# Attention and soft mixture of experts on one core: room for loads by the work of a block of instructions

## The chip, the cores and the metric

The kernel runs on one core of a Trainium2 chip. The metric is the time of one execution on the device in microseconds (us), the median over timed runs. A trace of one more execution was taken by the hardware profiler. TensorE, which multiplies matrices, appears there as PE (matmuls) and PEld (loads of weights); VectorE is DVE, ScalarE is ACT, GpSimd is POOL, and SyncE, whose queue issues every transfer of this kernel, is SP.

## What is computed

The first half is attention with a local window, for 8 batches and 8 heads of width 64: 512 local positions and 32 global ones.

```python
k_all = concatenate([k_g, k_l], axis=2); v_all = concatenate([v_g, v_l], axis=2)
s_g = scale * q_g @ k_all.T                     # 32 global rows see all keys
out_g = softmax(s_g) @ v_all
s_ll = where(abs(pos_q - pos_k) <= 32, scale * q_l @ k_l.T, -1e9)
s_l = concatenate([scale * q_l @ k_g.T, s_ll])  # local rows: global keys and a band
out_l = softmax(s_l) @ concatenate([v_g, v_l])
x = concatenate([out_g, out_l], axis=2)         # 4608 rows of 512
```

The second half is a soft mixture of 8 experts with 4 slots each, on all 4608 rows:

```python
logits = x @ phi                                # 4608 x 32
slot_input = softmax_over_rows(logits).T @ x    # 32 x 512
slot_out[e] = relu(slot_input[e] @ w1[e]) @ w2[e]
out = softmax_over_slots(logits) @ slot_out
```

## The kernel before, in words

The attention is a loop of 32 steps (L550), one for each pair of heads of a batch, four steps to a batch. A step makes the scores of its pair on TensorE, finishes the values of the pair two steps back, turns the exponentials of the pair one step back, and has parts of the logits, slot sums and global rows of earlier batches between them. Which of these a step has depends on its place in the batch, so the steps of a batch differ from one another, and each batch repeats the one before it. After the loop come the slots' experts: 64 pages of weights of 512 KB each (`w1` and `w2`, all of 32 MB), of which up to 30 have room of their own and can be loaded during the loop; the others follow after it, into room that the attention gives back. Then the results are combined and written out.

All loads are issued by SP, in the order of the program. The transfers of a load are held back by a wait on one TensorE instruction: `behind(d, i)` (L101) makes the load wait for instruction `i`. Which load waits for which instruction is settled while the program is built, by `begin_loads` (L105). TensorE's instructions are counted (`counted`, L89: a matmul in f32 counts 4, one in bf16 or a transpose 2, since each becomes that many loads of weights and matmuls), and each time the count passes a multiple of 256, `begin_loads` adds `ROOM` = 1040 KB to the room that is left and chooses a set of waiting loads. It takes all that are due by the next step and, beside them, up to three others, so that the sum of sizes comes as near to the room as it can, in classes of 200 KB. What is left over or overdrawn, up to 300 KB, goes to the next choice. A group of 256 TensorE instructions is called a **block** below.

The sizes in KB stand in the program: keys of two pairs (`k`) 736, values of two pairs (`v`) 780, queries of one pair (`q`) 256, global queries of a batch (`qg`) 64, a page of weights (`w`) 512. Each load has a due step, one step or more before its first use; loads of pages have none inside the loop.

Of the kernel before, what the change touches and what calls it, by code (L numbers as in the profile page):

```python
# [2 lines left out]

# [6 lines left out]
BF16 = mybir.dt.bfloat16  # L10
# [39 lines left out]
ROOM = 1040  # L50
SPARE = 300


def window(c):

    w = min(max(c, 1), 14)
    return ((w - 1) % 3, (w - 1) // 3)
# [9 lines left out]
def kernel(  # L67
# [12 lines left out]
    nc = tc.nc  # L80
# [4 lines left out]
    pe = [OFFSET]  # L85
    lines = [[], []]
    room, step = [0], [0]

    def counted(i, n):  # L89
        pe[0] += n  # L90
        if pe[0] // 256 > (pe[0] - n) // 256:
            begin_loads(i)
        return i

    def mm(out, lhsT, rhs, **flags):
        return counted(nc.tensor.matmul(out, lhsT, rhs, **flags), 2 if lhsT.dtype == BF16 else 4)  # L96

    def flip(out, x, idn):
        return counted(nc.tensor.transpose(out, x, idn), 2)  # L99

    def behind(d, i):  # L101
        tc.add_manual_dep(d.ins, i.ins.name, mybir.DependencyInfo(
            mybir.DependencyClass.Sync, mybir.DependencyReason.DATA))

    def begin_loads(i):  # L105

        lines[0].sort(key=lambda load: load[1])
        room[0] += ROOM
        near = [load for load in lines[0] if load[1] <= step[0] + 1]
        rest = [load for load in lines[0] if load not in near] + lines[1][:2]  # L110
        sets = [near + list(more) for n in range(4) for more in combinations(rest, n)]
        best = min(sets, key=lambda s: (abs(sum(load[0] for load in s) - room[0]) // 200, sum(load[1] for load in s)))
        for entry in best:
            lines[entry in lines[1]].remove(entry)
            room[0] -= entry[0]
            for d in entry[2]():
                behind(d, i)
        room[0] = max(min(room[0], SPARE), -SPARE)

    def begin_due(k):  # L120

        lines[0].sort(key=lambda load: load[1])
        while lines[0] and lines[0][0][1] <= k:
            size, due, load = lines[0].pop(0)
            room[0] -= size
            load()
# [111 lines left out]
    def scores(k):  # L238
        pool, tag = (psV, "v") if k == 1 else (psS, "s")
        ps = pool.tile([P, 2, 4, P], F32, tag=tag, name=f"s{k}")  # L240
        for i in (0, 2):
            for r in range(2):
                mm(ps[32 * i:32 * i + 64, r], idm[64 * r:64 * r + 64, :], mk[64 * r:64 * r + 64, i:i + 4, :],
                   start=True, stop=False)
        for t in range(4):
            for i in range(4):
                c = 4 * t + i
                for r in range(2):
                    mm(ps[32 * i:32 * i + 32, r, t, :], qs[k][64 * r:64 * r + 64, 32 * c:32 * c + 32],
                                     key_window(k, r, c), start=False, stop=(t == 3))  # L250
        sc[k] = ps
# [283 lines left out]
    def line_up(kind, j):  # L535
        if j < (B if kind == "qg" else NK) and (kind, j) not in lined:
            lined.add((kind, j))
            size, load = {"k": (736, load_k), "q": (256, load_q), "v": (780, load_v), "qg": (64, load_qg)}[kind]
            due = {"k": min(j - 1, NK - 3), "qg": min(4 * j + 2, NK - 3), "q": j - 1, "v": j + 1}[kind]
            lines[0].append((size, due, lambda: load(j)))  # L540
# [5 lines left out]
    def do_logits(b, pl):  # L546
        lgs[b] = new_logits(b)
        nc.scalar.copy(lgs[b][:, 0, :], pl)

    for k in range(NK):  # L550
        b, s = k // 4, k % 4
        step[0] = k
        begin_due(k)
        scores(k)
        line_up("q", k + 3)
        if k == 0:
            line_up("k", 4)
            line_up("v", 2)
            line_up("v", 4)
            line_up("qg", 0)  # L560
            lines[1].extend((512, NK, load_page) for _ in range(NWA))

        if k > 1:
            values(k - 2)
        shift(k)
        if k - 1 in GS:
            global_shift(GS.index(k - 1))
        if k - 2 in GS:
            global_values(GS.index(k - 2))
            for j in (k + 1, k + 3):  # L570
                line_up("v", j)
        if k in GS:
            global_scores(GS.index(k))
            line_up("qg", b + 1)
            for j in (k + 3, k + 5):
                line_up("k", j)
        if s == 0 and b > 1:
            slot_sums(b - 2)
        if s == 2 and b:
            pl = psT.tile([P, P], F32, tag="t", name=f"pl{b - 1}")  # L580
            logits_mm(pl, b - 1, range(4))
            do_logits(b - 1, pl)
        if k == 19:
            pl = psT.tile([P, P], F32, tag="t", name="plg")
            logits_g_mm(pl, 0)
            lgs["g", 0] = new_logits("g0")
            nc.scalar.copy(lgs["g", 0][G, 0, :], pl[G])
        if k == 21:
            pag = psT.tile([P, DM], F32, tag="t", name="pag")
            for g in range(2):  # L590
                slot_sums_g(0, pag, g)
        if k > 1:
            normalise(k - 2)
        if k in GS:
            global_max(GS.index(k))

        if k:
            transpose_exp(k - 1)
        if k - 1 in GS:
            global_transpose(GS.index(k - 1))  # L600
        if s == 3 and b:
            turn(b - 1, ALL)
        if k == 20:
            turn(("g", 0), G)
        if k == 18:
            turn_xg(0)
        if k > 2 and s != 2:
            turn_x(k - 3)
        if k > 2 and s == 1:
            turn_x(k - 2)  # L610
        if k == NK - 1:
            make_v(k)
        if k:
            make_v(k - 1)
        if k - 2 in GS:
            global_normalise(GS.index(k - 2))
        if s == 2 and b:
            dispatch_max(b - 1, ALL)
            dispatch_exp(b - 1, ALL)
        if s == 3 and b:  # L620
            dispatch_total(b - 1, ALL)
            combine_max(b - 1)
            combine_exp(b - 1)
        if k == 19:
            dispatch_max(("g", 0), G)
            dispatch_exp(("g", 0), G)
        if s == 0 and b > 1:
            add_sums(b - 2, pa[b - 2], ALL)
            combine_sum(b - 2, cTs[b - 2].rearrange("p (t s) -> p t s", s=NS))
        if k == 21:  # L630
            dispatch_total(("g", 0), G)
            add_sums(("g", 0), pag, G)
            combine_max(("g", 0))
            combine_exp(("g", 0))
        if k == 22:
            combine_sum(("g", 0), cg[:, 0:1, :])
# [85 lines left out]
    for g in range(2):  # L722
        c = slice(256 * g, 256 * g + 256)
        p = (pa7, pb7)[g]
# [228 lines left out]
```

## Time and profile before

| what | value |
|---|---|
| median of 3 timed runs (lowest to highest) | 278.23 us (277.56 to 280.18) |
| the profiled execution's own time | 276.72 us |
| its span, first to last instruction | 274.7 us |
| PE matmul busy | 247.9 us, 90% of the span |
| DVE, ACT, POOL busy | 167.3, 112.9, 98.6 us |
| transfers by SP's queue | 76.64 MB |
| mean rate of all transfers | 282 GB/s |
| chain of waits: PE / transfers / issue | 70% / 19% / 4% |

The span runs from the first to the last instruction of the program. A busy time is the time in which at least one instruction of that engine runs. "Issue" in the chain of waits is time in which an engine waited for nothing that the profile shows: no semaphore, no other engine, no transfer of the kernel's own. Transfers that fetch instructions for an engine are listed under queues of their own (q8 and q14), beside q1, which carries the kernel's data.

### The profile page before, as it was taken

Reading aid. Unit: us, or ns where it says so; the run is one execution under the profiler, and the core shown is the slowest. Engines: PE = TensorE matmul, PEld = TensorE weight load, DVE = VectorE, ACT = ScalarE, POOL = GpSimd, SP = SyncE. Lnnn points to the kernel's source line nnn. Section 1 sums busy time; section 2 is a strip of 40 time slices with the busy share of each in tenths; the row PEclk is TensorE's granted clock in tenths of the full one; section 3 lists DMA queues with packets and bytes.
Section 4 is the critical chain, followed back from the end, with each engine's and each line's share of the span. In section 5 each row is a group of like instructions: output and inputs, shape, how many; then the busy total and the mean of one; then the engine's idle time right before and its main releaser. Section 6 shows DMA issues by size and latency. Waiting matters only on the chain.

```text
span 274.7 us, 13972 instructions
## 1 busy us (share of the span) xinstructions
PE 247.9 (90%) x6348; PEld 174.3 (63%) x6348; DVE 167.3 (61%) x336; ACT 112.9 (41%) x254; POOL 98.6 (36%) x174
## 2 busy tenths in 40 slices
PE   7599989999999899899999989989899999998740
PEld 5477856777687577777777866758786344553520
DVE  0769757767967695596789767858554234044440
ACT  0317425623644483357337426726454001133330
POOL 0345654454546436334555563435710000000000
PEclk9979999999999999999999999999999999999995
DMA  7967786768677867695867496687789999999997
GB/s 216 391 222 248 230 296 209 259 222 296 199 242 262 296 206 237 229 333 168 285 218 292 146 342 205 233 237 255 243 278 412 409 410 407 410 407 383 351 353 253
DMA packets 29275, 77.53 MB, mean 282 GB/s; under 512 B 2592, under 2 KB 12192, under 8 KB 29216
## 3 DMA queue, kind: packets, MB, share of 16 engines
q1 hardware_dynamic: 29216, 76.64, 79.3%
q8 instruction: 50, 0.82, 1.2%
q14 instruction: 9, 0.07, 0.1%
HBM read 67.72 MB, written 8.91 MB: 279 GB/s over the span
## 4 chain that ended last, share of the span: by engine, by line
PE 70%; DMA 19%; issue 4%; DVE 1%; ACT 1%; SPq 0%
DMA w<-in_w_dram 18%; PE s L96 17%; PE o L96 14%; PE t L99 12%; PE xt L99 5%; PE og L96 4%; PE tg L99 3%; PE gm L96 3%; PE pl L96 3%; PE pc L96 2%; PE pa L96 2%; DMA con<-in_cst_dram 1%; PE gs L96 1%; ACT o L828 1%; PE po L96 1%
## 5 line engine op out<-in xcount | busy, mean ns | idle before, releaser
L258 DVE TENSOR_REDUCE mx<-s 128x8 f32<-128x1024 f32 x32 | 39.1, 1223 | 42.3 <-PE s L96 42.2
L222 POOL COPY va<-v 128x650 f32<-128x650 f32 x31 | 22.5, 726 | 82.5 <-PE o L96 67.6
L270 ACT ACTIVATE e<-t 128x512 f32<-128x512 f32 x64 | 35.0, 599 | 41.4 <-PE t L99 41.2
L260 DVE TENSOR_TENSOR e<-s,mx 128x1024 f32<-128x1024 f32 x32 | 39.2, 1225 | 6.6 <-PE o L96 2.3
L96 PE MATMUL s<-k,q 64*32 64x128 f32 x2048 | 38.8, 276 | 4.8 <-issue 4.1
L96 PE MATMUL o<-v,e 128*32 128x65 f32 (+1 forms) x640 | 42.0, 224 | 0.0
L96 PE MATMUL o<-va,e 128*64 128x65 f32 (+1 forms) x620 | 39.6, 225 | 0.0
L96 PEld LDWEIGHTS s<-k,q 64*32 64x32 f32 x2048 | 29.3, 106 | 13.2 <-issue 12.1
L96 PEld LDWEIGHTS o<-v,e 128*32 128x32 f32 (+1 forms) x640 | 33.1, 115 | 6.5 <-issue 5.5
L99 PE MATMUL t<-con,e 128*128 128x128 f32 x256 | 36.2, 285 | 1.0 <-issue 0.5
L99 PEld LDWEIGHTS t<-con,e 128*128 128x128 f32 x256 | 28.1, 143 | 13.0 <-ACT sg L320 5.9
L96 PEld LDWEIGHTS o<-va,e 128*64 128x64 f32 (+1 forms) x620 | 31.8, 115 | 2.1
L96 PE MATMUL o<-vb,e 128*32 128x65 f32 x496 | 27.8, 221 | 1.8 <-issue 1.8
L96 PEld LDWEIGHTS o<-vb,e 128*32 128x32 f32 x496 | 22.2, 109 | 2.5 <-issue 2.5
L300 DVE TENSOR_TENSOR xh<-o,r 128x512 f32<-128x512 f32 x32 | 22.1, 691 | 1.9 <-PE pa L96 0.5
L223 POOL COPY va<-v 32x650 f32<-32x650 f32 x31 | 22.3, 719 | 1.9
L224 POOL COPY vb<-v 64x520 f32<-64x520 f32 x31 | 19.1, 618 | 1.8
L225 POOL COPY vb<-v 64x520 f32<-64x520 f32 x31 | 18.9, 611 | 1.7
L99 PE MATMUL xt<-con,xh 128*128 128x128 f32 x128 | 19.1, 278 | 0.3 <-ACT e L270 0.2
L384 ACT COPY xT<-xt 128x512 f32<-128x512 f32 x32 | 18.6, 606 | 0.6 <-PE xt L99 0.4
L828 DVE COPY o<-pc 128x512 f32<-128x512 f32 x16 | 10.3, 686 | 11.5 <-PE pc L96 11.5
L828 ACT COPY o<-pc 128x512 f32<-128x512 f32 x16 | 8.6, 589 | 20.7 <-PE pc L96 20.7
(179 smaller groups left out, 367.5 us busy)
## 6 DMA issues: line engine op xcount, KB each, us to landing
w<-in_w_dram SPq DMA_DIRECT2D x64, 512.0 KB, 8.1
v<-in_vS_dram SPq DMA_DIRECT2D x15, 780.0 KB, 5.0
k<-in_kT_dram SPq DMA_DIRECT2D x14, 736.0 KB, 5.5
q<-in_qT_dram SPq DMA_DIRECT2D x32, 256.0 KB, 3.4
out_dram<-o SPq DMA_DIRECT2D x16, 512.0 KB, 6.4
k<-in_kT_dram SPq DMA_DIRECT2D x4, 368.0 KB, 5.4
v<-in_vS_dram SPq DMA_DIRECT2D x2, 390.0 KB, 6.5
qg<-in_qG_dram SPq DMA_DIRECT2D x8, 64.0 KB, 2.3
```

Source lines behind the costliest of these rows:

```text
L96: return counted(nc.tensor.matmul(out, lhsT, rhs, **flags), 2 if lhsT.dtype == BF16 else 4)
L99: return counted(nc.tensor.transpose(out, x, idn), 2)
L222: nc.gpsimd.tensor_copy(va, v[:, 0:5])
L223: nc.gpsimd.tensor_copy(va[0:32], v[0:32, 1:6])
L224: nc.gpsimd.tensor_copy(vb[64:128], v[64:128, 0:4])
L225: nc.gpsimd.tensor_copy(vb[0:64], v[0:64, 1:5])
L258: nc.vector.reduce_max(mx, ps, axis=AX.X)
L260: nc.vector.tensor_tensor(e, ps, bc(mx, P), ALU.subtract)
L270: nc.scalar.activation(es[k][:, r], pt, AF.Exp, scale=SCALE)
L300: nc.vector.tensor_tensor(xhs[u][:, :, P * pp:P * pp + P].rearrange("p t (r d) -> p r t d", r=2), o[:, :, :, 0:D], bc(rc, D), ALU.mult)
L384: nc.scalar.copy(xTs[k], pt)
L828: (nc.vector.tensor_copy if t % 2 else nc.scalar.copy)(dst, src)
```

## The change

In each block from step 9 on, the room that is added is `ROOM * share()` in place of `ROOM`. `share()` compares work: every matmul adds its columns (weighted by type and by the part of the array that it uses) to a running sum, a transpose a fixed 330. The block that lies one batch (four steps) back, at the same place of its batch, is compared with that batch's mean block; two thirds of the ratio and one third of one make the share. Before step 9 the share is one.

```diff
+TURN = 330
@@
-    def counted(i, n):
+    work, begun = [(0, 0)], {}
+
+    def counted(i, n, columns):
         pe[0] += n
+        work.append((pe[0], work[-1][1] + columns))
         if pe[0] // 256 > (pe[0] - n) // 256:
             begin_loads(i)
         return i
 
     def mm(out, lhsT, rhs, **flags):
-        return counted(nc.tensor.matmul(out, lhsT, rhs, **flags), 2 if lhsT.dtype == BF16 else 4)
+        rows, wide = lhsT.shape[0], lhsT.shape[1]
+        columns = math.prod(out.shape[1:]) * (1 if lhsT.dtype == BF16 else 4) * min(rows, 128) * wide / 128 ** 2
+        return counted(nc.tensor.matmul(out, lhsT, rhs, **flags), 2 if lhsT.dtype == BF16 else 4, columns)
 
     def flip(out, x, idn):
-        return counted(nc.tensor.transpose(out, x, idn), 2)
+        return counted(nc.tensor.transpose(out, x, idn), 2, TURN)
+
+    def share():
+        k = step[0]
+        if k < 9:
+            return 1
+        period = begun[k] - begun[k - 4]
+        upto = lambda p: next(w for at, w in work if at >= p)
+        p = pe[0] - period
+        own = (upto(p + 256) - upto(p)) / (upto(begun[k]) - upto(begun[k - 4])) * period / 256
+        return (1 + 2 * own) / 3
@@
-        room[0] += ROOM
+        room[0] += ROOM * share()
@@
     for k in range(NK):
         b, s = k // 4, k % 4
         step[0] = k
+        begun[k] = pe[0]
```

No instruction of PE, DVE, ACT or POOL is added, removed or moved. What moves is the order of the loads on SP's queue and the TensorE instruction that each waits for. Three places follow; the times are those at which TensorE reaches the blocks in the trace of the kernel before. Names are buffers by number: `k_`, `q_`, `v_`, `qg_` as above, `w_` a pair of pages; "x2" is two equal rows.

SP's queue at the blocks that begin at 97.07, 102.91 and 105.53 us (a long block, a short one and one between). Before: q, k and qg in the first; q and two pages in the second; k and q in the third.

```order
L198 DMA q_2179<-in_qT_dram 128x512
L194 DMA k_2181<-in_kT_dram 128x1472
L202 DMA qg_2183<-in_qG_dram 128x128
L198 DMA q_2299<-in_qT_dram 128x512
L175 DMA w_2301<-in_w_dram 128x1024 x2
L194 DMA k_2374<-in_kT_dram 128x1472
L198 DMA q_2376<-in_qT_dram 128x512
```

Now: two k in the first; qg, q and one page in the second; two pages in the third.

```order
L215 DMA k_2180<-in_kT_dram 128x1472
L215 DMA k_2182<-in_kT_dram 128x1472
L223 DMA qg_2298<-in_qG_dram 128x128
L219 DMA q_2300<-in_qT_dram 128x512
L196 DMA w_2062<-in_w_dram 128x1024
L196 DMA w_2373<-in_w_dram 128x1024 x2
```

So 416 KB more are asked for in the first block (1472 in place of 1056), 448 KB fewer in the second (832 in place of 1280), 32 more in the third.

SP's queue at the blocks that begin at 123.71, 129.43 and 132.35 us, again long, short and long. Before: k and q; qg and two pages; k and q.

```order
L194 DMA k_2790<-in_kT_dram 128x1472
L198 DMA q_2792<-in_qT_dram 128x512
L202 DMA qg_2911<-in_qG_dram 128x128
L175 DMA w_2913<-in_w_dram 128x1024 x2
L194 DMA k_2986<-in_kT_dram 128x1472
L198 DMA q_2988<-in_qT_dram 128x512
```

Now: two k; qg, q and one page; q and one page.

```order
L215 DMA k_2789<-in_kT_dram 128x1472
L215 DMA k_2791<-in_kT_dram 128x1472
L223 DMA qg_2910<-in_qG_dram 128x128
L219 DMA q_2912<-in_qT_dram 128x512
L196 DMA w_2591<-in_w_dram 128x1024
L219 DMA q_2985<-in_qT_dram 128x512
L196 DMA w_2987<-in_w_dram 128x1024
```

The first block has 480 KB more (1472 in place of 992), the second 256 fewer (832 in place of 1088), the third 224 fewer (768 in place of 992).

SP's queue at the blocks that begin at 186.74, 189.68 and 195.42 us, and the first pages after the loop. Before: v and one page in the first block, two pages in the second, two in the third (the pairs straddle the blocks), and the last page of `w_4427` with `w_4539` after the loop.

```order
L210 DMA v_4235<-in_vS_dram 128x1560
L175 DMA w_4237<-in_w_dram 128x1024 x2
L175 DMA w_4335<-in_w_dram 128x1024 x2
L175 DMA w_4427<-in_w_dram 128x1024 x2
L175 DMA w_4539<-in_w_dram 128x1024 x2
```

Now: v alone in the first, two pages in each of the others, and the pair `w_4536` with `w_4539` after the loop.

```order
L231 DMA v_4235<-in_vS_dram 128x1560
L196 DMA w_4332<-in_w_dram 128x1024 x2
L196 DMA w_4424<-in_w_dram 128x1024 x2
L196 DMA w_4536<-in_w_dram 128x1024 x2
L196 DMA w_4539<-in_w_dram 128x1024 x2
```

Up to `v_4235` 24 pages are begun in both programs; the page that stood beside it is now begun after the loop. So the loop begins 28 pages in place of 29, and 36 are left for after it in place of 35.

Other blocks whose sum changes by more than 60 KB, by the time at which they begin (KB now, and before): 54.25 (832, 1056), 66.03 (1292, 1036), 74.25 (992, 1056), 80.12 (1088, 1024), 87.17 (780, 1036), 110.84 (1036, 780), 115.30 (768, 1280), 149.17 (1248, 736), 158.57 (780, 1292), 167.29 (1280, 1024), 171.98 (1312, 1056). The blocks that begin at 70.62, 83.65, 137.99, 141.52, 146.13, 155.04, 163.20, 177.83 and 180.99 ask for the same sums as before.

## Rows read from the trace of the kernel before

**Rows 1.** The page: busy time of each engine; the queue of fetched instructions (packets, MB).

```profile
PE 247.9 (90%) x6348; PEld 174.3 (63%) x6348; DVE 167.3 (61%) x336; ACT 112.9 (41%) x254; POOL 98.6 (36%) x174
...
q8 instruction: 50, 0.82, 1.2%
```

**Rows 2.** The chain of waits in order of time: start, length, what.

```profile
109.75 1.09 issue
...
161.83 1.36 issue
```

**Rows 3.** One block each: us, PE, PEld, DVE, ACT, POOL busy, PEclk, DMA, GB/s.

```profile
54.25:57.44 3.19, 2.54 (x151) 2.11 (x134) 2.32 (x2) 0.00 (x0) 1.21 (x2) 1.00 0.18 55
57.44:62.30 4.86, 4.68 (x127) 3.71 (x127) 2.35 (x8) 2.05 (x4) 2.62 (x7) 1.00 0.89 331
...
70.62:74.25 3.63, 3.47 (x131) 2.33 (x130) 3.46 (x8) 2.86 (x7) 0.83 (x2) 1.00 0.43 105
...
83.65:87.17 3.52, 3.25 (x130) 2.32 (x129) 1.78 (x3) 1.01 (x3) 1.54 (x6) 1.00 0.71 226
87.17:92.37 5.20, 4.27 (x128) 3.24 (x127) 3.53 (x7) 1.92 (x6) 2.32 (x4) 1.00 0.90 309
...
102.91:105.53 2.62, 2.57 (x140) 2.14 (x136) 1.31 (x2) 0.36 (x1) 0.61 (x2) 1.00 0.39 88
105.53:110.84 5.31, 4.22 (x127) 3.41 (x127) 2.62 (x7) 2.06 (x4) 3.62 (x8) 1.00 0.96 339
...
115.30:117.94 2.64, 2.64 (x133) 2.11 (x130) 1.57 (x4) 1.08 (x4) 0.51 (x2) 1.00 0.39 85
...
129.43:132.35 2.92, 2.62 (x150) 2.19 (x137) 2.11 (x2) 0.00 (x0) 0.96 (x2) 1.00 0.30 68
...
155.04:158.57 3.53, 3.53 (x142) 3.23 (x132) 3.19 (x8) 1.08 (x3) 2.62 (x4) 1.00 0.19 53
158.57:163.20 4.63, 3.27 (x131) 2.33 (x129) 2.86 (x5) 1.01 (x3) 2.59 (x7) 1.00 0.97 352
...
177.83:180.99 3.16, 2.56 (x141) 2.13 (x137) 1.85 (x2) 0.37 (x1) 1.12 (x2) 1.00 0.56 172
...
189.68:195.42 5.74, 5.03 (x129) 4.01 (x127) 3.38 (x7) 3.16 (x9) 4.78 (x8) 1.00 0.86 322
195.42:199.79 4.37, 4.30 (x128) 3.74 (x129) 3.34 (x11) 1.93 (x4) 3.15 (x6) 1.00 0.67 211
sum 150.91, PE 143.97 PEld 109.16 DVE 111.02 ACT 76.45 POOL 76.76; mean PE 4.23 PEld 3.21 DVE 3.27 ACT 2.25 POOL 2.26
```

**Rows 4.** Transfers in the block from 105.53 until 108.5 us: packets, MB, share.

```profile
q1 hardware_dynamic: 263, 0.89, 91.5%
```

**Rows 5.** Fetched instructions from 108.5 to 109.6 us, the same block.

```profile
q8 instruction: 1, 0.02, 5.3%
```

**Rows 6.** Data from 101.9 to 102.7 us, the end of a long block.

```profile
q1 hardware_dynamic: 120, 0.25, 81.7%
```

**Rows 7.** Transfers from 102.7 to 104.2 us.

```profile
q1 hardware_dynamic: 84, 0.07, 14.1%
q8 instruction: 1, 0.02, 5.9%
```

**Rows 8.** Transfers from 129.8 to 131.0 us.

```profile
q8 instruction: 1, 0.02, 5.1%
q1 hardware_dynamic: 7, 0.01, 2.7%
```

**Rows 9.** The chain of waits after the loop, first and last of five such pieces.

```profile
200.40 7.66 DMA w<-in_w_dram
...
240.23 10.10 DMA w<-in_w_dram
```

**Rows 10.** A stretch after the loop, columns as in rows 3.

```profile
206.00:250.37 44.37, 43.01 (x514) 21.04 (x506) 14.70 (x45) 9.53 (x26) 1.03 (x3) 1.00 1.03 407
```

**Rows 11.** The page: transfers by issuing instruction: count, KB each, us to landing.

```profile
v<-in_vS_dram SPq DMA_DIRECT2D x15, 780.0 KB, 5.0
k<-in_kT_dram SPq DMA_DIRECT2D x14, 736.0 KB, 5.5
```

More of the change, by code (lines that the diff above doesn't have):

```diff
@@ L1 @@
+import math
 from contextlib import ExitStack
```

## The prediction

> **What bounds the kernel now.** I read the page first, then the chain of waits in order of time, then a table of stretches, one for each block of 256 TensorE instructions, and last the transfers inside single stretches.
>
> The page shows TensorE busy for 247.9 of 274.7 us, with 6348 loads of weights and 6348 matmuls, and a queue of its own that brought 50 packets, 0.82 MB in all, so 16 KB each [rows 1]. 12,696 instructions over 50 packets are 254 a packet: each packet is one block of 256 instructions for TensorE. In the chain some pieces are "issue": TensorE stood still and waited for nothing that the profile shows [rows 2]. Counted over the trace, both of these pieces end at the same number of TensorE instructions modulo 256. So I cut the loop at that number. From 48.88 to 199.79 us this gives 34 stretches of 150.91 us together, in which PE is busy for 143.97 [rows 3]: 6.9 us are lost there, nearly all at the ends of blocks. A stretch's loss is its length less its PE time [rows 3]: 0.65 us at 54.25, 0.18 at 57.44, 0.16 at 70.62, 0.27 at 83.65, 0.93 at 87.17, 1.09 at 105.53, 0.30 at 129.43, 1.36 at 158.57, 0.60 at 177.83, 0.71 at 189.68.
>
> What is waited for is the next block. In the stretch from 105.53 no instruction packet runs until 108.5, while data moves with 91.5% of the engines' time [rows 4]; then one comes, 0.053 x 16 engines x 1.1 us = 0.93 us long, before 109.6 [rows 5], and PE goes on at 110.84 [rows 2], 1.24 us or more after it. At the start of the block before, data had run with 81.7% of the engines until 102.7 [rows 6] and then all but stopped (14.1%); the packet came right at the edge, between 102.7 and 104.2 [rows 7], and only 0.05 us were lost. At 129.43 the packet had 0.01 MB beside it [rows 8]. So the packet for the next block begins when TensorE enters a block, stands behind data asked for in the **block before**, and its lateness is paid at the end of the block entered, if that block is too short to hide it. With an empty queue a block of some 2.6 us of PE work is at the limit: 0.05, 0.00, 0.30 and 0.65 us are lost at 102.91, 115.30, 129.43 and 54.25 [rows 3].
>
> After the loop the chain is the transfer of pages, five pieces from 200.40 to 250.33 [rows 9], with the engines full and 407 GB/s [rows 10]. That is the price of bytes: 512 KB are 0.524 MB, 1.29 us; 256 KB 0.64; 64 KB 0.16.
>
> **The change, part by part.** TensorE's work stays, so the PE times of the blocks stay. Three things move.
>
> *Blocks that ask for less*, ahead of a block that now ends late. 54.25 asks for 224 KB less (0.56 us), which frees the 0.18 us lost at 57.44. 102.91 asks for 448 KB less (1.13 us): the 1.09 us at 105.53 go. 186.74 asks for 512 KB less (1.29 us): the 0.71 us at 189.68 go. Sum -1.98 us, and nothing at the other end, if each packet stood behind other data; I take the whole, since each cut in bytes is longer than the loss behind it. The other lighter blocks (74.25, 87.17, 115.30, 129.43, 132.35, 158.57) stand ahead of blocks that lose nothing from this cause, and give nothing.
>
> *Blocks that ask for more*, ahead of a block with little to spare. In full, by 407 GB/s, the packet is later by: 0.64 us in 70.62 (256 KB more in 66.03), 0.16 in 83.65, 1.05 in 102.91 (416 KB), 0.64 in 115.30, 1.21 in 129.43 (480 KB), 1.29 in 155.04 (512 KB), 0.64 in 177.83. That is 5.63 us at most, and none at least, if the queue is empty anyway by the time the packet is due. My values by block, estimates between these ends: 0.8 of 1.05 in 102.91, ahead of which data ran until 102.7 [rows 6]; 0.1 of 1.21 in 129.43, where 0.01 MB moved beside the packet and the queue had been dry [rows 8]; 0.4 in 155.04, whose 3.53 us of PE are 0.9 above the limit of 2.6 [rows 3] and hide that much; and about half in the other four, whose queue I see only through their mean rates of 85 to 226 GB/s [rows 3]: 0.25 in 70.62, 0.15 in 83.65, 0.35 in 115.30, 0.45 in 177.83. Sum +2.5 us. Time lost so lets the queue drain: 0.4 us at 155.04 come off the 1.36 lost at 158.57, and 0.15 at 83.65 off the 0.93 lost at 87.17, together -0.55.
>
> The blocks at 83.65, 155.04 and 177.83 are short but keep their sums, because pages and values come in lumps of 512 and 780 KB. So the two largest losses of this kind that stand behind them (0.93 and 1.36) are touched only by what drains, and the 0.65 at 54.25 not at all.
>
> *One page fewer in the loop.* It moves from 186.74, where the engines had room, to the stream after the loop, which is full from 206 on. There it costs its whole transfer: +1.29 us. The least is nothing, if the idle third of the engines just before the stream (0.67 busy from 195.42 [rows 3]) took it in; but the page waits for a TensorE instruction at the end of that stretch, so I take the whole.
>
> At nothing I cost loads that start later. A key load lands 5.5 us after its issue and values 5.0 [rows 11]; each is still begun by its due step, a step or more ahead of use, and a step is (199.79 - 54.25) / 23 = 6.3 us, about 23 steps lying between these edges. If one came late, TensorE would wait for a transfer inside the loop, which it never does now.
>
> Sum: -1.98 + 2.5 - 0.55 + 1.29 = **+1.3 us**. On the profiled execution's own 276.72 us that is 278.0. This execution lies 1.51 us below the median of the runs shown, 278.23; I add the difference to the median: **279.5 us**.
>
> **The rivals.**
>
> *Relief alone.* The heavier blocks are long, 4.5 to 5.9 us, and the data is through before the next edge. For it: the dry queue at 129.43 [rows 8]. Against it: data ran until 102.7 [rows 6], 0.2 us before the edge, with 416 KB less to bring. Then -1.98 + 1.29 = -0.7: 277.5 us.
>
> *The wait moves into the short blocks: slower.* At the end of a short block there is no cover at all; if the queue passes on every byte, the heavier blocks cost 5.63 less the 0.9 hidden at 155.04, and drain 0.55. Then -1.98 + 4.73 - 0.55 + 1.29 = +3.5: 281.7 us. This decides from the point where 70% of those bytes reach the packet.
>
> *The queue of data doesn't delay the packet.* Then the losses have another cause and stay. For it: 0.65 us are lost at 54.25 with data at 55 GB/s [rows 3]. Against it: the packet that didn't run before 108.5 [rows 4]. The losses stay and the page alone counts: +1.29, 279.5 us. The Trainium skill, "DMA: Bandwidth & Descriptors", section "Queues, rings and completion order", says that each DMA engine takes turns between the queues that have work, packet by packet, so a fetch would wait for one packet and not for a backlog. By that rule the first two terms would be zero and the sum +1.29; the trace speaks against it, with a wait of some 3 us for the packet in the stretch from 105.53.
>
> *The change evens out what it means to.* Its share is taken from columns, not from time, and from the block at the same place one batch ago; if the lumps happened to fit, all ten losses would fall, by up to 6 us. Against it: the list of sums, in which three of the short blocks ahead of or among the losses don't change.
>
> **How the numbers follow.** Forecast, within 1 us of 279.5: 0.50. Relief alone: 0.18. Wait in the short blocks: 0.20. Queue of no effect: 0.08. All losses fall (273.5): 0.04. The range goes from a little below relief alone, 276.9, to the full price, 281.7. About 1% is what a measurement of this kernel can tell from no change, 275.4 to 281.0 here. Faster by over 1%: the last rival, 0.04, and 0.01 from relief. Slower by over 1%: most of the wait in the short blocks, 0.16, and the upper edge of the forecast, 0.06: 0.22. Within: 0.73.
>
> **What would show it.** In the profile after: "issue" at 105.53 and 189.68 (by the blocks' new times) below 0.3 us; new issue of 0.5 us or more at the end of the block of 102.91, and more than 0.6 at that of 177.83; 0.9 to 1.4 us still there at 87.17 and 158.57; the pages' stream after the loop 1.3 us longer from the loop's end to its own. Wrong would be: blocks of 2.6 us without a loss behind blocks of 1472 KB, a stream of the same length, or TensorE waiting for q, k or v inside the loop.

## The result, and the profile after

The changed kernel takes 279.91 us (median of 21 runs, 277.32 to 282.80), the kernel before 278.23 (21 runs in all by then). The ratio is 1.0062, its 95% interval 1.0037 to 1.0086: 1.73 us slower, between 1.03 and 2.39. Ratios here leave out runs that lie more than 1.5% above the fastest of the same kernel; medians take all runs, and six of the later traces are of such longer runs (pages moved out of the way, cuts alone, page back, the better table's first, and both other rules). The profiled execution took 279.09 us, its span is 277.1.

The page of the changed kernel, the busy times and the shares of the chain:

```profile
PE 249.8 (90%) x6347; PEld 175.3 (63%) x6348; DVE 167.6 (60%) x336; ACT 112.9 (41%) x254; POOL 98.7 (36%) x174
...
PE 71%; DMA 17%; issue 4%; DVE 3%; ACT 1%; SPq 0%; DVEq 0%
```

The work is the same as in [rows 1]. PE's busy time is 1.9 us longer: 0.65 ahead of the stretches below, 0.45 in them (144.42 for 143.97) and 0.80 behind them (61.85 for 61.05). Keys and values land as fast as in [rows 11] (5.4 and 4.9 us), and TensorE waits for no q, k or v inside the loop. The pieces of "issue" of 0.4 us and more between 86 and 190 us in its chain of waits (start, length), to be held against [rows 2]:

```profile
86.42 1.91 issue
...
106.98 1.38 issue
...
119.49 0.46 issue
...
134.07 0.54 issue
...
164.96 1.12 issue
...
183.15 1.09 issue
```

One stretch for each block that the prediction speaks of, in the trace of the changed kernel (columns as in [rows 3]; the sum is that of all 34 blocks from 49.02 to 201.83):

```profile
54.39:57.28 2.89, 2.55 (x151) 2.12 (x134) 2.02 (x2) 0.00 (x0) 0.90 (x2) 1.00 0.19 61
57.28:61.68 4.40, 4.39 (x127) 3.59 (x127) 2.19 (x8) 2.05 (x4) 2.92 (x7) 1.00 0.98 351
...
83.16:88.33 5.17, 3.26 (x131) 2.32 (x129) 3.37 (x6) 1.01 (x3) 3.07 (x8) 1.00 1.01 350
88.33:93.93 5.60, 5.60 (x126) 4.34 (x129) 1.28 (x4) 2.02 (x6) 0.79 (x2) 0.70 0.50 162
...
104.41:108.36 3.95, 2.57 (x140) 2.14 (x136) 2.61 (x4) 0.36 (x1) 1.84 (x3) 1.00 0.64 190
108.36:112.30 3.94, 3.94 (x126) 3.40 (x127) 1.42 (x5) 2.06 (x4) 2.39 (x6) 1.00 0.81 268
...
116.76:119.95 3.19, 2.73 (x134) 2.10 (x130) 2.12 (x4) 1.08 (x4) 0.36 (x1) 1.00 0.65 179
...
131.44:134.60 3.16, 2.63 (x150) 2.19 (x137) 2.35 (x2) 0.00 (x0) 1.20 (x2) 1.00 0.31 79
...
157.65:161.71 4.06, 3.70 (x143) 3.26 (x133) 3.47 (x8) 1.56 (x3) 2.80 (x5) 1.00 0.69 208
161.71:166.08 4.37, 3.25 (x128) 2.32 (x127) 2.37 (x3) 0.59 (x1) 2.16 (x6) 1.00 0.90 311
...
180.60:184.24 3.64, 2.55 (x140) 2.12 (x136) 2.34 (x2) 0.36 (x1) 1.59 (x3) 1.00 0.80 259
...
192.66:197.42 4.76, 4.76 (x132) 3.90 (x130) 2.97 (x7) 3.16 (x9) 4.47 (x7) 1.00 0.64 236
...
sum 152.81, PE 144.42 PEld 109.82 DVE 110.55 ACT 76.03 POOL 76.79; mean PE 4.25 PEld 3.23 DVE 3.25 ACT 2.24 POOL 2.26
```

A loss is again a stretch's length less its PE time. In order these are, by the block's start in the trace before: 54.25, 57.44, 83.65, 87.17, 102.91, 105.53, 115.30, 129.43, 155.04, 158.57, 177.83, 189.68. The losses of [rows 3] at 105.53 (1.09) and 189.68 (0.71) are gone: 3.94 of 3.94, 4.76 of 4.76. In their place the short blocks ahead of them lose: 1.38 us at 102.91, where it was 0.05, and 1.09 at 177.83, where it was 0.60. At 83.65 it is 1.91 in place of 0.27. All 34 blocks lose 8.39 us; before it was 6.94.

The packet's time tells the same of the block of 102.91. In [rows 7] it came right at the edge. Now, from 104.41 to 105.9 us, only data runs:

```profile
q1 hardware_dynamic: 66, 0.29, 47.8%
```

and the packet comes in the next stretch, from 105.9 to 107.0 us, 1.5 us or more into the block:

```profile
q1 hardware_dynamic: 161, 0.15, 65.7%
q8 instruction: 1, 0.02, 5.3%
```

TensorE goes on at 108.36, 1.36 us after 107.0. The data took less than half of the engines' time in the first of these stretches; which engine brings the packet, the views don't show.

After the loop, a stretch of the stream of pages, then all from the start of the block of 199.79 to the end; behind that the same from the kernel before:

```profile
208.00:252.54 44.54, 43.13 (x516) 21.17 (x514) 15.03 (x45) 9.68 (x27) 1.04 (x3) 1.00 1.02 402
...
201.83:277.10 75.27, 61.85 (x778) 33.38 (x777) 26.02 (x66) 18.40 (x43) 1.82 (x6) 0.93 1.00 373
```

```profile
199.79:274.70 74.91, 61.05 (x779) 33.30 (x777) 25.91 (x66) 18.40 (x43) 1.81 (x6) 0.96 0.99 372
```

The engines are nearly as full as in [rows 10] (402 GB/s for 407), and the end stands some 0.4 us further from the loop's last blocks in this pair of traces.

### The profile page after: what moved, and what is told of

It is laid out like the page before. It is cut to its first block, busy times and chain, and to the rows that moved or that the text cites. A ratio compares the mean times of both kernels' runs of the same rounds, so it can differ in the third digit from the quotient of the medians.

```text
span 277.1 us, 13968 instructions
## 1 busy us (share of the span) xinstructions
PE 249.8 (90%) x6347; PEld 175.3 (63%) x6348; DVE 167.6 (60%) x336; ACT 112.9 (41%) x254; POOL 98.7 (36%) x174
## 4 chain that ended last, share of the span: by engine, by line
PE 71%; DMA 17%; issue 4%; DVE 3%; ACT 1%; SPq 0%; DVEq 0%
PE s L106 17%; DMA w<-in_w_dram 15%; PE o L106 14%; PE t L109 11%; PE xt L109 6%; PE og L106 3%; PE pl L106 3%; PE tg L109 3%; PE gm L106 3%; PE pa L106 3%; PE pc L106 2%; DMA con<-in_cst_dram 2%; DVE e L281 1%; PE gs L106 1%; DVE mx L279 1%
## 5 line engine op out<-in xcount | busy, mean ns | idle before, releaser
L106 PEld LDWEIGHTS s<-k,q 64*32 64x32 f32 x2048 | 29.9, 108 | 9.7 <-issue 9.7
```

## The experiments

The theory: a packet of 256 instructions for TensorE is fetched behind the data asked for in the block before, and what it is late is lost at the end of the block entered. The rivals: the fetch does not stand behind data (another cause for the losses); and, for the changed kernel, a theory of which edit costs what. All losses below are named by the block's start in the trace before.

In most experiments the program's choice is replaced by a table that lists, for each block, the loads that it begins, as (KB, due step). With the table of the kernel before it is that kernel; then single entries are moved:

```diff
-        sets = [near + list(more) for n in range(4) for more in combinations(rest, n)]
-        best = min(sets, key=lambda s: (abs(sum(load[0] for load in s) - room[0]) // 200, ...
-        for entry in best:
+        for size, due in TABLE.get(pe[0] // 256, ()):
+            entry = next(e for line in lines for e in line if e[:2] == (size, due))
```

**Three pages moved, nothing else.** In the kernel before, one page each goes from 102.91, 129.43 and 158.57 into the long block ahead of a short one (97.07, 123.71, 149.17). `w` is a page, (512, 32).

```diff
-    21: [(256, 17), (736, 17), (64, 18)],
-    22: [(256, 18), w, w],
+    21: [(256, 17), (736, 17), w],
+    22: [(64, 18), (256, 18), w],
-    27: [(736, 21), (256, 22)],
-    28: [(64, 22), w, w],
+    27: [(736, 21), (256, 22), w],
+    28: [(64, 22), w],
-    33: [(736, 27)],
-    35: [(780, 27), w],
+    33: [(736, 27), w],
+    35: [(780, 27)],
```

> The kernel before with three pages of weights moved from a short block into a long block ahead of a short one; all else as before. By block (begin in the trace of before, us): 97.07 asks for 1504 KB in place of 1056 and 102.91 for 832 in place of 1280; 123.71 for 1504 in place of 992 and 129.43 for 576 in place of 1088; 149.17 for 1248 in place of 736 and 158.57 for 780 in place of 1292. Theory A (the fetch of the next block's instructions stands behind data asked for in the block before, and is paid for at the end of the block entered): the loss at the end of the block of 102.91 goes from 0.05 to 1.0 to 1.5 us, at 129.43 from 0.30 to 0.5 to 1.3, at 155.04 from 0 to 0.3 to 0.8, and the 1.09 lost at 105.53 falls below 0.3. Rival B (a turn for each queue, the fetch waits for no backlog): each of these losses stays within 0.3 us of what it was.

Measured: 276.35 us in one run. The blocks of 102.91, 105.53, 129.43, 155.04 and 158.57:

```profile
102.81:106.26 3.45, 2.58 (x141) 2.15 (x137) 2.14 (x2) 0.36 (x1) 1.38 (x3) 1.00 0.50 185
106.26:111.01 4.75, 4.21 (x127) 3.40 (x127) 1.80 (x7) 2.05 (x4) 2.86 (x7) 1.00 0.99 339
...
129.60:132.52 2.92, 2.63 (x150) 2.20 (x137) 2.11 (x2) 0.00 (x0) 0.96 (x2) 1.00 0.54 170
...
155.77:159.83 4.06, 3.70 (x142) 3.27 (x133) 3.47 (x8) 1.56 (x3) 2.80 (x5) 1.00 0.80 278
159.83:163.66 3.83, 3.25 (x128) 2.32 (x128) 1.82 (x2) 0.59 (x1) 1.69 (x5) 1.00 0.80 237
```

Loads decide where the loss falls. Behind 448 KB more, 102.91 loses 0.87 us where it lost 0.05, and 155.04 loses 0.36 behind 512 KB more where it lost nothing. A fetch that didn't stand behind data would have left both as they were. The first is clear of chance: in seven other traces without more data ahead 102.91 never loses over 0.21. The second is not: with the same 512 KB more in the change's traces 155.04 loses 0.36, nothing and 0.09. The other two doses missed: 512 KB more ahead of 129.43 changed nothing (0.29; before, 0.30), and behind 448 KB less 105.53 still loses 0.55. It was to fall below 0.3, and the kernel with five pages fewer (below) loses the same 0.55 there behind unchanged loads, so this fall from 1.09 shows nothing. 158.57 loses 0.58 in place of 1.36, but nothing was taken out ahead of it: the page left the block of 158.57 itself.

**Pages moved out of the way.** In the kernel before, five loads that stand ahead of a losing block go elsewhere, four pages and one q: pages from 102.91 to 117.94, from 155.04 to 163.20, from 186.74 to 43.70, from 80.12 to 92.37, and the q for step 15 from 83.65 to 80.12.

```diff
-    17: [w, w],
-    18: [(256, 15), (780, 15)],
+    17: [(256, 15), w],
+    18: [(780, 15)],
-    22: [(256, 18), w, w],
+    22: [(256, 18), w],
-    34: [(64, 26), (256, 26), (256, 27), w],
+    34: [(64, 26), (256, 26), (256, 27)],
-    36: [(780, 29)],
+    36: [(780, 29), w],
-    41: [(780, 31), w],
+    41: [(780, 31)],
...
```

> The kernel before with four pages of weights moved out of blocks ahead of a loss (80.12, 102.91, 155.04, 186.74) into blocks ahead of a long block (92.37, 117.94, 163.20, 43.70), and one load of queries moved from 83.65 to 80.12; 29 pages in the loop as before. Theory A: the losses at 87.17, 105.53, 158.57 and 189.68 (4.1 us in all) fall to less than 1.0 together, no new loss over 0.3 comes, and the time falls by 2.5 to 4 us, to a ratio of 0.986 to 0.991. Rival B: the losses stay and the ratio is 0.997 to 1.003. Rival C (a moved load costs as much where it goes): the old losses fall and new ones of the same sum come at the ends of the blocks that follow 92.37, 117.94, 163.20 and 43.70; ratio 0.997 to 1.003.

Measured: 277.55 us (6 runs) against 279.06; ratio 0.9893 (0.9815 to 0.9970). At 87.17, 105.53 and 189.68 nothing is lost any more (0.92, 1.09 and 0.71 before), and 158.57 loses 0.82 (1.36 before). But 83.65 lost 1.09, and a new loss came behind the page put into 163.20, in the block of 167.29, which lost nothing in any other trace:

```profile
167.13:173.33 6.20, 5.03 (x128) 3.22 (x127) 4.95 (x11) 3.77 (x10) 2.67 (x4) 1.00 0.83 318
```

6.20 less 5.03 is 1.17 us, behind 1292 KB in a block of 4 us: a relief has to be put where the next block can bear it.

**Five pages fewer in the loop.** The kernel before, with room for 24 pages in place of 29 in the loop; the loads before the first page that is left out are the same.

```diff
-            lines[1].extend((512, NK, load_page) for _ in range(NWA))
+            lines[1].extend((512, NK, load_page) for _ in range(NWA - 6))
```

> The kernel before with five pages of weights fewer begun in the loop (24 in place of 29, the last five left out there and begun after it). Theory A (a page after the loop costs its whole transfer): from the start of the block of 199.79 to the end of the span 74.9 us become 81.3 (five times 1.29 more). Rival D (the stream after the loop has room at its start, as the changed kernel's 0.4 us for one page suggests): 2 us more or less, 75 to 77. In both, the 0.71 us lost at 189.68 go.

Measured: 282.16 us in one run. From the start of the block of 199.79 to the end, and the block of 189.68, which now stands behind 780 KB in place of 1292:

```profile
200.25:280.10 79.85, 64.13 (x778) 33.80 (x777) 25.92 (x66) 18.40 (x43) 1.82 (x6) 0.94 1.00 376
...
191.08:195.84 4.76, 4.76 (x126) 3.91 (x129) 2.42 (x7) 3.16 (x9) 4.48 (x7) 1.00 0.27 108
```

Three traces with 29 pages (the kernel before, the three pages moved, and the kernel before once more, below) have 74.91, 75.13 and 73.79 us there, 74.61 in the mean. So five pages cost 79.85 - 74.61 = 5.24 us, 1.05 a page: between the two forecasts, less than the transfer of one (1.29), and no page is free in the mean. The loss at 189.68 is gone with the page ahead of it, as in the change.

**The small load first.** In the changed kernel the block of 80.12 begins three loads, qg and two pages. Here qg goes one block earlier.

```diff
-    16: [(256, 14), (736, 15)],
-    17: [(64, 14), w, w],
+    16: [(64, 14), (256, 14), (736, 15)],
+    17: [w, w],
```

> The changed kernel with one load of 64 KB (global queries) begun one block earlier, so that the block of 80.12 issues two loads and not three. Theory E (the third issue of a block comes more than a microsecond late and with it the data ahead of the next fetch): the loss at the end of the block that follows, 1.91 us in the changed kernel, falls below 0.7. Theory A by bytes alone: 64 KB are 0.16 us, so it stays at about 1.75. Rival F (chance from run to run): anything between.

Measured: 278.30 us in one run. The block of 83.65:

```profile
82.61:87.23 4.62, 3.25 (x131) 2.32 (x129) 2.85 (x5) 1.00 (x3) 2.59 (x7) 1.00 0.79 270
...
101.75:104.30 2.55, 2.55 (x141) 2.14 (x137) 1.25 (x2) 0.35 (x1) 0.55 (x2) 1.00 0.35 76
```

It loses 1.37 us with two loads ahead of it; the changed kernel lost 1.91 with three. So it doesn't take a third load to make this loss. Whether late issues make it is not settled: here too SP's issues last until 2.29 us into the block of 80.12, for 2.56 in the change (last section). The second line is 102.91: behind the same 1472 KB as in the change it loses nothing here.

**The cuts alone.** In the changed kernel the raises at 97.07, 110.84, 149.17, 167.29 and 171.98 are taken back (those at 66.03, 80.12 and 123.71 stay), and so is the cut at 158.57; the other cuts are kept. The loads that this sets free go to 43.70, 92.37 and 117.94, which a long block follows. It still has 28 pages.

```diff
-    21: [(736, 17), (736, 19)],
+    21: [(256, 17), (736, 17)],
-    33: [(736, 27), w],
-    35: [(780, 27)],
+    33: [(736, 27)],
+    35: [(780, 27), w],
-    38: [(256, 29), (64, 29), (736, 29), (256, 30)],
+    38: [(64, 29), (736, 29), (256, 30)],
...
```

> The changed kernel with its raised blocks put back: the blocks of 97.07, 110.84, 149.17 and 171.98 ask again for what they asked before (992, 780, 736 and 1056 KB), and the loads set free go to blocks ahead of long ones; the cut blocks (54.25, 102.91, 186.74) stay cut; 28 pages in the loop as in the change. Theory A: the losses that the change brought at the ends of the blocks of 102.91, 115.30, 155.04 and 177.83 (3.4 us together in its trace) fall back to less than 1.4, those at 105.53 and 189.68 stay below 0.5, and the kernel is 1 to 2.5 us faster than the change: a ratio to before of 0.995 to 1.001. Rival G (the change's loss is the page after the loop, not the raised blocks): the ratio stays at 1.003 to 1.009.

Measured: 277.85 us (12 runs) against 278.81; ratio 1.0004 (0.9957 to 1.0050). The blocks of 102.91 and 177.83:

```profile
102.93:105.48 2.55, 2.55 (x140) 2.14 (x137) 1.25 (x2) 0.36 (x1) 0.55 (x2) 1.00 0.23 51
...
180.35:183.23 2.88, 2.56 (x139) 2.13 (x136) 1.57 (x2) 0.37 (x1) 0.89 (x2) 1.00 0.41 127
```

With the raises taken back, 102.91 loses nothing (1.38 in the change), 177.83 loses 0.32 (1.09), 155.04 nothing (0.36). So the raises are what these blocks lost by. It is not so clear elsewhere: 115.30 loses 0.73 without its raise (0.46 in the change's first trace), 105.53 loses 0.59, which was to stay below 0.5, 158.57 loses 1.91, and the loop as a whole loses 8.04 us where the change's first trace lost 8.39. In time the middle agrees, no slower than before without them, but not the whole interval: it reaches to 1.0050, and the change's own starts at 1.0037.

**The page back.** The changed kernel with one more page in 117.94, 29 in all.

```diff
-    26: [(780, 21), (256, 21)],
+    26: [(780, 21), (256, 21), w],
```

> The changed kernel with one more page of weights begun in the block of 117.94, so that 29 are begun in the loop as before. Theory H (the stream after the loop takes the first page into its idle start): the time from the start of the block of 199.79 to the end falls by 0 to 0.5 us and the ratio to before stays at 1.003 to 1.008. Rival G (the page costs its whole transfer): 1.3 us less, a ratio of 0.999 to 1.004.

Measured: 279.46 us (13 runs) against 278.81; ratio 1.0023 (0.9969 to 1.0076). By the medians 0.45 us below the change, by the ratios 1.1; the interval holds both no effect and a full page. Not settled by time. In its one trace, of a run of 284.73 us, the stretch from the start of the block of 199.79 to the end takes 74.46 us; the change has 75.32 there in the mean of three traces. That is 0.86 less, between the two forecasts, and no more than single traces differ by.

**The better table.** The table of moved pages, with the page that cost 1.17 us taken out of 163.20 and put into 167.29.

```diff
-    36: [(780, 29), w],
-    37: [(256, 28), (256, 29), w],
+    36: [(780, 29)],
+    37: [(256, 28), (256, 29), w, w],
```

> The table of the second experiment, with the page that it put into the block of 163.20 (where a new loss of 1.2 us came behind it) put into the block of 167.29 instead, ahead of the longest block. Theory A: the loss behind 163.20 goes, no new one comes behind 167.29, and the ratio to before is 0.985 to 0.992. Rival C (a moved load costs as much where it goes): 0.996 to 1.002.

Measured: 274.68 us (6 runs, 272.62 to 276.71) against 278.81; ratio 0.9860 (0.9781 to 0.9939). The loss at 167.29 is gone. This beats the kernel before, and the change's 279.91 by 5.2 us.

**The kernel before and the change, once more.** No edit; each again with a trace, to see which losses come back at the same ends.

> The kernel before once more, unchanged, for its trace. Theory A with chance: the losses at 105.53, 158.57, 87.17 and 54.25 come again at the same ends of blocks, each within 0.6 us of the first trace, and those behind long blocks (102.91, 115.30, 155.04) stay below 0.4. Rival F (chance alone): the losses come at the ends of other blocks.

> The changed kernel once more, unchanged, for its trace. Theory A: losses at the ends of the blocks of 83.65, 102.91, 115.30 and 177.83 come again, 3 to 7 us together, none over 0.2 at 189.68. Rival F (chance alone): they come at other places.

Measured: 276.59 and 279.30 us, one run each. The blocks of 102.91, 105.53, 115.30 and 177.83, first in the kernel before:

```profile
100.90:103.26 2.36, 2.36 (x139) 2.09 (x137) 1.18 (x1) 0.36 (x1) 0.40 (x1) 1.00 0.23 61
103.26:109.07 5.81, 4.37 (x143) 3.42 (x131) 2.76 (x8) 2.07 (x4) 3.84 (x8) 1.00 0.96 377
...
113.53:116.99 3.46, 2.73 (x133) 2.10 (x130) 2.39 (x4) 1.08 (x4) 1.27 (x3) 1.00 0.37 99
...
178.22:181.56 3.34, 2.55 (x141) 2.12 (x137) 2.04 (x2) 0.36 (x1) 1.20 (x3) 1.00 0.68 222
```

then in the change:

```profile
101.74:104.78 3.04, 2.57 (x140) 2.14 (x136) 1.73 (x2) 0.36 (x1) 1.03 (x2) 1.00 0.46 155
104.78:110.09 5.31, 4.21 (x127) 3.41 (x127) 2.21 (x7) 2.05 (x4) 3.20 (x8) 1.00 0.89 326
114.55:118.56 4.01, 2.73 (x133) 2.11 (x130) 2.91 (x6) 1.08 (x4) 1.81 (x3) 1.00 0.86 334
...
180.77:184.43 3.66, 2.56 (x141) 2.12 (x137) 2.36 (x2) 0.36 (x1) 1.61 (x3) 1.00 0.81 255
```

Most losses come at the same ends, but not in the same size, and some come at others: in the kernel before 115.30 lost 0.73 here, where it was to stay below 0.4, and 186.74 lost 0.81, and neither lost anything the first time; in the change 105.53 lost 1.10 and 146.13 lost 1.21, where the first trace had none. With the same loads one block varies by about half a us, and up to 1.2, and the loop as a whole by 2 us and more (6.94 and 8.80 lost in the kernel before, 8.39 and 11.04 in the change). A term must therefore be read from several traces.

These four traces also show the link itself, over their 136 blocks. Call **outstanding** what SP had begun to issue and what had not yet come when TensorE entered a block. With less than 100 KB outstanding the packet begins 0.6 us into the block, in the mean; with 500 to 700 KB 1.5 us; above 900 KB 2.8 us; single blocks lie about half a us to either side. At all 36 ends that lose 0.3 us or more TensorE goes on 1.2 to 1.6 us after the packet's end. Packets take about 0.9 to 1.4 us, so a block of 2.5 us of PE time can lose something even with the queue empty: 54.25 lost 0.33 us in the repeat of the kernel before, with nothing outstanding.

**The share from the next block.** The rule of the change, but the share is the work of the block that will have to bear the load, one later than the one that begins it.

```diff
-        own = (upto(p + 256) - upto(p)) / (upto(begun[k]) - upto(begun[k - 4])) * period / 256
+        own = (upto(p + 512) - upto(p + 256)) / (upto(begun[k]) - upto(begun[k - 4])) * period / 256
```

> The changed kernel with one line altered: the share of a block is taken from the work of the block after it (the one at whose end a late fetch is paid for), not from its own; 28 pages in the loop. Theory A: blocks ahead of short ones ask for less, blocks ahead of long ones for more, so the losses at the ends of the short blocks (102.91, 115.30, 155.04, 177.83) fall below those of the changed kernel (3.4 us in its trace) to 1.5 or less, and the ratio to before is 0.990 to 1.000, below the change's 1.006. Rival C (the lumps of 512 to 780 KB decide, whatever the rule): 1.002 to 1.008.

Measured: 279.25 us (12 runs) against 278.56; ratio 1.0079 (1.0029 to 1.0129). The blocks of 102.91 and 105.53:

```profile
106.07:108.61 2.54, 2.54 (x140) 2.14 (x136) 1.23 (x2) 0.36 (x1) 0.44 (x2) 1.00 0.29 69
108.61:114.53 5.92, 4.22 (x131) 3.40 (x127) 2.71 (x7) 2.05 (x4) 3.71 (x8) 1.00 0.80 295
```

The short block is spared, as the rule means it, and the next one loses 1.70 us. The whole is not better than the change.

**The mean of both blocks, in full.** The share is the mean of own and next block's work, with no third of one in it.

```diff
-        own = (upto(p + 256) - upto(p)) / (upto(begun[k]) - upto(begun[k - 4])) * period / 256
-        return (1 + 2 * own) / 3
+        own = (upto(p + 512) - upto(p)) / 2 / (upto(begun[k]) - upto(begun[k - 4])) * period / 256
+        return own
```

> The changed kernel with the share taken in full from the mean work of a block and the one after it, since both lengths are there to bring the data and to hide the fetch; 28 pages in the loop. Theory A: 0.988 to 0.998. Rival C (lumps decide): 1.002 to 1.008.

Measured: 278.79 us (12 runs) against 278.56; ratio 1.0009 (0.9965 to 1.0053). No gain on the kernel before, and the interval reaches into the change's. It still loses 1.09 us at 102.91 and 1.64 at 105.53.

**The better table, once more.** No edit, beside other runs of the kernel before.

> The table of the third round once more (ratio 0.986 there, with an interval from 0.978 to 0.994). Theory A: 0.982 to 0.992 again. Rival F (chance): 0.995 or above.

Measured: 275.67 us (6 runs, 273.38 to 278.09) against 278.56; ratio 0.9881 (0.9811 to 0.9952). The blocks of 87.17, 102.91, 105.53, 177.83 and 189.68:

```profile
88.32:92.36 4.04, 4.04 (x126) 3.17 (x129) 2.68 (x7) 1.92 (x6) 2.24 (x4) 1.00 0.85 259
...
102.84:105.19 2.35, 2.35 (x139) 2.08 (x138) 1.18 (x1) 0.36 (x1) 0.40 (x1) 1.00 0.38 87
105.19:109.56 4.37, 4.37 (x143) 3.42 (x131) 2.76 (x8) 2.07 (x4) 3.64 (x8) 1.00 0.98 367
...
177.18:179.57 2.39, 2.39 (x141) 2.12 (x137) 1.22 (x1) 0.36 (x1) 0.41 (x2) 1.00 0.32 63
...
188.53:193.30 4.77, 4.76 (x127) 3.91 (x130) 2.43 (x7) 3.16 (x9) 4.48 (x7) 1.00 0.54 184
```

Five blocks that lose in the kernel before or in the change lose nothing or 0.01 us here. The loop loses 4.64 us (5.32 in this table's first trace), 1.48 of it at 54.25, against 8.03 in the mean of three traces (the kernel before, its repeat, five pages fewer): 3.4 us, where the medians give 2.9.

## Why the prediction was right, and where its terms were not

The forecast was 279.5 us, +1.3 on the kernel before; 279.91 and +1.73 were measured. The mechanism held. The sizes of its terms did not, and in part they made up for one another: that the sum came out so near is partly luck. The table takes the mean loss of three traces on either side: the kernel before, its repeat and the one with five pages fewer (for 189.68 the first two); the change, its repeat and the one with qg earlier. The ends of the stream come from the kernel before, its repeat and the three moved pages, against the same three of the change.

| term | block: us before, after | sum | forecast |
|---|---|---|---|
| less ahead | 57.44: 0.17, 0.06; 105.53: 1.03, 0.75; 189.68: 0.57, 0 | -0.96 | -1.98 |
| more ahead | 70.62: 0.12, 0.15; 83.65: 0.36, 1.64; 102.91: 0.03, 0.62; 115.30: 0.31, 1.10; 129.43: 0.54, 0.54; 155.04: 0, 0.15; 177.83: 0.64, 1.28 | +3.48 | +2.5 |
| drain | 87.17: 1.01, 0; 158.57: 1.54, 1.29 | -1.26 | -0.55 |
| one page | 74.61, 75.32 | +0.71 | +1.29 |
| all | | +1.97 | +1.3 |

Taken over the whole loop, the same six traces lose 8.03 and 9.40 us in the mean; with the page that is +2.1.

*Blocks that ask for less.* "I take the whole" was the step that failed. At 189.68 it held, in the change and with five pages fewer. At 105.53 the loss came back in two of three traces of the change (1.10 and 1.15), with 832 KB ahead in place of 1280. In the first trace 102.91 stood still for 1.38 us ahead of it, and 464 KB were outstanding as TensorE entered 105.53; in the other two, where 102.91 lost 0.47 and nothing, it was 716 and 760. Where 97.07 isn't raised and 102.91 has 768 KB (the tables with moved pages, three traces) 105.53 loses nothing; with the cuts alone, 832 KB and no raise, it lost 0.59. So a cut of 448 KB stands near the edge there and does not take the whole.

*Blocks that ask for more.* Five of the seven values came out within 0.3. At 129.43 the dry queue [rows 8] was the right row to go by: 480 KB more cost nothing there, nor did 512 in the first experiment. At 115.30 the value was too low (+0.79, forecast 0.35). The one that was far off is 83.65, 0.15 said and 1.28 measured, for 64 KB more. This is no price of 64 KB: the loss of 1.01 at 87.17 moved one block ahead, and the two together rose only from 1.37 to 1.64. What changed is how much was outstanding as TensorE entered 83.65: 545, 557 and 469 KB in the three traces before; 865 and 861 in the change, where the small qg stands ahead of the two pages in SP's queue and the packet began 2.75 and 2.47 us into the block in place of 1.2 to 1.5. So what is priced must be what is outstanding at the edge, not what one block asks for. That is not all of it: with qg earlier 589 KB were outstanding, and the packet still began 2.20 us in. What decides the rest is open.

*Drain.* Of the 1.01 at 87.17 all went, where 0.15 was said, since the block before it now stands still while the queue empties (186 and 247 KB outstanding as TensorE enters it in the change, 803 and 777 before); at 158.57 it was 0.25 for 0.4.

*One page.* "So I take the whole" was too much: 0.71 us between the traces, 1.05 a page for five of them. For the first page the engines' idle third before the stream may count, as the prediction held open (they are 0.92 busy in the change's last block of the loop, 0.67 before), and the later ones cost nearly all of their 1.29. Single traces there differ by 1.3 us before and by 1.2 after, which is more than the term.

Of the rivals, *relief alone* fell with the losses at 102.91, 115.30 and 177.83. *The wait moves into the short blocks* is what happened in kind: it priced the raises at 4.73 less 0.55 of drain, and 3.48 less 1.26 came. *All losses fall* was never near. *The queue of data doesn't delay the packet* was put at 279.5 as well, so the time alone could not tell it from the forecast. The first experiment does: its count of instructions and pages is that of the kernel before, and the loss at 102.91 came behind the data that was added; and in the four traces of the two kernels the packet comes the later the more is outstanding. By the Trainium skill, "DMA: Bandwidth & Descriptors", section "Queues, rings and completion order", the engines take turns between queues with work, and a fetch would wait for one packet of data, of 9 to 17 descriptors as a rule. Whether this case's traces disagree hangs on how long such a packet is: if the records of 5888 bytes that a load of keys leaves in them, 0.22 us each on one engine, are its descriptors, then by an estimate from the section's count one packet takes 2.0 to 3.8 us, and the 0.82 us that 102.91 lost more behind 448 KB would fit. That the delay goes on growing, to 2.8 us above 900 KB, speaks for the whole of the data and not one packet; no run here sets the two apart.

Of what would show it, the losses at 102.91, 177.83 and 158.57 came as said (1.38, 1.09 and 1.12), those at 105.53 and 189.68 went as said in the first trace, and the one at 87.17 went though it was to stay. A stream 1.3 us longer was said, and it was 0.4 in that pair of traces. One sign of being wrong came too, in one trace of three: with qg earlier 102.91 lost nothing behind 1472 KB, with 163 KB outstanding where the other two had 405 and 393.

Why the change doesn't gain is shown by the cuts and raises in the table, and at 102.91 and 177.83 by the cuts alone; how much of the time each is worth is within the noise of single traces. A block's room is paid for by the block after it. The rule gives long blocks more, and short ones follow them: 102.91 behind 97.07, 177.83 behind 171.98. Giving the share to the right block doesn't mend it by itself (1.0079 and 1.0009): a choice among lumps of 256 to 780 KB with room carried over misses any smooth share by more than the share changes. That last point is argued, from the fact that neither rule gains on the kernel before and a table set by hand does twice.

## What to carry to other kernels

Where an engine stands still for "issue" at equal counts of its instructions, cut the trace at that count, and count what is outstanding at each cut: here it delayed the instructions for the next block. So put large loads into blocks that a long block follows, one load at a time, and look for the loss that each move makes elsewhere. A rule of shares is worth little while its lumps are as large as a block's room. A term of half a us needs several traces of the same program.

## What the runs showed of the hardware

Behind some of the longest losses TensorE's clock was granted at half, the 1.2 GHz level, for 3.4 us. In the change's first trace this followed the 1.91 us: the block of 87.17 took 5.60 us of PE time at a mean granted clock of 0.70 (above), where it has 4.27 in [rows 3] and 4.04 in the change's repeat. From 88.60 on:

```profile
88.60:92.00 3.40, 3.40 (x41) 2.66 (x30) 0.55 (x3) 0.91 (x3) 0.58 (x1) 0.50 0.56 161
```

So a loss of 1.91 us can cost most of its length again behind it as PE time, 1.33 to 1.56 us here, and losses read as length less PE time don't count that. With the page back it followed 3.00 us of standing still:

```profile
171.90:175.30 3.40, 3.40 (x66) 2.63 (x72) 0.50 (x2) 1.97 (x6) 0.00 (x0) 0.50 0.70 225
```

It followed 1.91 us with the cuts alone and 1.71 with the share from the next block too, but not 2.19 us in the trace with five pages fewer, 2.18 with the pages moved out of the way, or 1.93 at 83.65 with the page back. What decides it is open.

Some of SP's issues take much longer than others. First SP in the change's first trace, in the block of 80.12, which begins at 79.63 there (start, length, operation); then the two pages of the same block in the kernel before, where it begins at 80.12, and with qg earlier, where it begins at 79.08:

```profile
80.12 0.33 SPq L223 DMA_DIRECT2D qg<-in_qG_dram  x1
80.50 1.69 SPq L196 DMA_DIRECT2D w<-in_w_dram  x2
...
80.61 0.81 SPq L175 DMA_DIRECT2D w<-in_w_dram  x2
...
79.57 1.80 SPq L213 DMA_DIRECT2D w<-in_w_dram  x2
```

The three issues of 64, 512 and 512 KB take until 82.19, 2.56 us into the block; the second page is issued 2.12 us into it. The same two pages alone take until 81.42, 1.30 us into the block, in the kernel before, and until 81.37, 2.29 us into it, with qg earlier. What makes an issue long is open.
